# Loads limited to five in flight, two more chunks stacked and one weight tile converted another way, in a linear attention with a gated feed-forward layer

## The chip, the core and the metric

The kernel runs on one core of a Trainium2 chip. A core has five engines with their own instruction queues: TensorE (PE) multiplies matrices, VectorE (DVE), ScalarE (ACT) and GpSimd (POOL) work elementwise, and SyncE (SP) issues nearly all transfers between memory and the core's buffers. PE's weight loads are shown apart as PEld. What counts is the time of one execution in device microseconds; lower is better. An execution's own time is a little more than the span of its trace.

## What is computed

```python
# attention: batch 4, heads 8, 768 tokens, head size 48
for t in range(S):
    kt, vt, rt = k[:, :, t], v[:, :, t], r[:, :, t]
    cur = einsum('bhd,bhe->bhde', u * kt, vt)
    y[:, :, t] = einsum('bhd,bhde->bhe', rt, state + cur)
    state = w * state + einsum('bhd,bhe->bhde', kt, vt)
# feed-forward on x = y with the heads side by side: width 384, 1024 hidden
h = maximum(x @ w_in, 0)
u, v = h[..., :512], h[..., 512:]
v_n = (v - mean(v)) / sqrt(var(v) + 1e-6)
v_s = einsum('ts,bsd->btd', w_spatial, v_n) + b_spatial
out = (u * v_s) @ w_out
```

The two weights w_in and w_out come as 64-bit numbers, all else as 32-bit ones.

## The kernel before

The 4 batches of 768 tokens are cut into 24 chunks of 128 tokens (`m`), six for each batch. A chunk is loaded in four pieces: `rk` (r and k with the head dimension on the partitions), `rs`, `ks` (r and k with tokens on the partitions) and `rkv` (v). `prep` scales them on POOL and DVE, `scores` and `products` multiply in 16 small fp32 matmuls each (two PE records a matmul), `state` carries the recurrence, and `apply` forms the chunk's rows of x in PSUM tile `xp`; `fin` splits x into a high and a low part. The first `FIRST_CHUNKS` chunks come in one form (tensor `rkvE`): `apply` then runs 36 or 48 small matmuls, separately for the carried state and the own chunk, and `block` copies the state into the tile `A` kept for that. The later chunks are stacked (tensor `rkvL`): the state is copied into `rkv`, r and the scores are copied side by side into a tile `A` (`move`, which ACT, DVE or a transfer on SP can do), and `apply` needs 32 matmuls.

The feed-forward products use a high and a low part of each operand, three matmuls a product (`mm3`): `moe_v` and `moe_u` multiply x by w_in, `moe_sp` the normalised v by w_spatial, `moe_out` the gated tile by w_out. w_in is loaded in six tiles (`wa`, three for v first) and w_spatial in six (`wb`); all w_spatial tiles are split into two parts ahead of the first `moe_sp`. `from_f64` (line 459) makes the two parts of a 64-bit weight tile. For tiles in `SUM_IN` (the first three of w_in) it sums three terms in three PE matmuls (lines 479 to 481), for the others it adds on DVE (lines 486, 488, 490).

Which engine does a task, and in which order each engine's instructions stand, is decided while the program is built, by `Plan` (line 118). It keeps a clock for each engine, buffers and the transfers, and takes the ready task with the earliest start, by due times. `SEEDS` shakes these due times and the leanings by random amounts, once for each seed. `Fetch` and `landing` are its models of PE's instruction loading and of loads. `lane` (line 208) lets the planner's loads start no earlier than the eighth last has landed. On the chip SP's queue is in order: a load that waits for its buffer or for an earlier transfer holds whatever stands behind it.

Of the kernel before, what the change touches and what calls it, by code (L numbers as in the profile page):

```python
# [25 lines left out]
NK = DM // P  # L26
# [6 lines left out]

OK, OV = DM, 2 * DM
ROW_E, ROW = OV + 2 * NP * 2 * D, OV + 2 * 2 * NP * HC
FIRST_CHUNKS = 8
SUBS = ((0, 64, 0), (1, 0, 64))


# [1 line left out]
AHEAD = 0.3  # L41
ALONE = 1000.0
CALM, LATE = 80.0, dict(DVE=1.0, SP=1.0)
SEEDS = (286629, 121708, 598343, 820393, 863996, 502042, 154941, 497759, 664270, 626866, 362431, 249003, 459248,
# [4 lines left out]
BIAS = dict(DVE=3.0, ACT=3.5)  # L49
MOST_IN, MOST_OUT = 2, 1  # L50

# [3 lines left out]
CHAIN = dict(PE=0.0, DVE=0.115, ACT=0.11, POOL=0.0, SP=0.0)  # L55
SWITCH = {"bs": 0.095, "br": 0.095, "by": 0.095, "sb": 0.215, "sy": 0.11, "rb": 0.105, "yb": 0.105}
STAY = 1.0
PORT = dict(DVE=(0.07, 0.0, 0.0), POOL=(0.15, 0.06, 0.02))


class Way:
    def __init__(self, engine, cost, emit, two=False, nbytes=0, lean=0.0, behind=None):
        self.engine, self.cost, self.emit, self.two, self.nbytes = engine, cost, emit, two, nbytes
        self.lean = lean + BIAS.get(engine, 0.0)
        self.behind = BEHIND[engine] if behind is None else behind
# [30 lines left out]
class Fetch:  # L96


    FIRST, BLOCK, BASE, SLOPE, MOST = 91, 128, 3.15, 0.5, 2.6

    def __init__(self):
        self.done, self.ready = 0, 0.0
# [15 lines left out]
class Plan:  # L118
# [1 line left out]

    RATE, SLOW, FIRST_BYTE, LANES = 400e3, 210e3, 1.2, 8

    def __init__(self, slots):
        self.slots = {k: [(0.0, i) for i in range(n)] for k, n in slots.items()}
        self.hold = []
        self.slot, self.turn, self.order, self.given, self.since = {}, {}, {}, {}, {}
        self.tasks, self.wrote, self.read, self.users = [], {}, {}, {}
# [41 lines left out]
    def shake(self):  # L171
        for seed in SEEDS:
            rnd = random.Random(seed)
            share, size = rnd.choice((0.01, 0.03, 0.1, 0.3)), rnd.choice((1.0, 3.0, 8.0))
            width, at = rnd.choice((3.0, 12.0, 50.0, 1000.0)), rnd.uniform(-10.0, 330.0)
            for t in self.tasks:
                if abs(t.due - at) < width and rnd.random() < share:
                    t.due += rnd.uniform(-size, size)
                    for w in t.ways:
                        w.lean += rnd.uniform(-size, size)  # L180
# [14 lines left out]
    def shared_cost(self, way, at):  # L195
        if not way.two:
            return way.cost
        lead, gap, tail = PORT[way.engine]
        return max(way.cost, self.port + gap - at + way.cost - lead)
# [6 lines left out]
    AHEAD_IN = 25.0  # L206

    def lane(self, at, landed):
        return max(at, landed[-self.LANES]) if len(landed) >= self.LANES else at

    def run(self):
        self.dues()
# [5 lines left out]
        free, line, landed, clock, fetch, bank = {}, 0.0, [], Clock(), Fetch(), {}  # L218
        self.port, self.kind = 0.0, "b"
        while ready:  # L220
            best, ahead = {}, dict(free)
            for t in sorted(ready, key=lambda t: (t.due, t.place)):
# [7 lines left out]
                for way in t.ways:  # L230
# [4 lines left out]
                    at = max(can, ahead.get(e, 1.0)) if len(t.ways) > 1 else max(can, free.get(e, 1.0))  # L235
                    if way.nbytes:
                        at = max(self.lane(at, landed), t.due - self.AHEAD_IN)
# [3 lines left out]
                _, e, can, way = found  # L241
                at = max(can, free.get(e, 1.0))
                if way.nbytes:
                    at = max(self.lane(at, landed), t.due - self.AHEAD_IN)
                if can <= ahead.get(e, 1.0) + AHEAD and not way.nbytes:
                    ahead[e] = max(can, ahead.get(e, 1.0)) + way.cost
                late = at <= free.get(e, 1.0) + 0.02
                due = t.due - STAY if e == "PE" and (t.kind == "b") == (self.kind == "b") else t.due
                key = (0, due, t.place) if late else (1, at, due, t.place)
# [5 lines left out]
            _, at, t, way = best[e]  # L255
# [6 lines left out]
            if way.two:  # L262
                self.port = at + cost - PORT[e][2]
            if e == "PE":
# [20 lines left out]
            for a in t.after:  # L285
                left[a] -= 1
                if not left[a]:
                    ready.append(a)
            way.emit()
        assert all(t.end is not None for t in self.tasks)  # L290


# [1 line left out]
def fused_kernel(ctx, tc, rkT, rkvE, rkvL, wT, uB, w_in, w_sp, b_sp, w_out, out):  # L294
    nc = tc.nc
    E = mybir.EngineType
    for e in (E.PE, E.DVE, E.Activation, E.Pool, E.SP):
        ctx.enter_context(tc.manual_schedule(engines={e}))
    EARLY, STATS, EC = 13, 1, FIRST_CHUNKS
    QUIET = 6  # L300
    CLASSIC = (0,)
    SUM_IN, SUM_OUT = range(NK), []
    LOAD_IN = {0: -50.0, 1: -50.0}
    SLOTS = dict(rk=2, rs=2, ks=2, rkv=3, a=1, A=2, t=4, X=2, gt=4, u=8, vs=2, g=3, ob=2, pm=5, ps=1, xp=1, x=2, s=2, t1=1, dg=2, q=2)
    SLOTS |= {f"w{x}{n}": 1 for x in "ab" for n in range(NS)}
    const = ctx.enter_context(tc.tile_pool(name="const", bufs=1))
    sbuf = ctx.enter_context(tc.tile_pool(name="sbuf", bufs=1))
    psum = ctx.enter_context(tc.tile_pool(name="psum", bufs=1, space=bass.MemoryType.PSUM))
    plan = Plan(SLOTS)
    T = {}  # L310

    def tile_of(key, shape, dtype=F32):
        key = key[:2]
        if key not in T:
            home = psum if key[0] in ("pm", "ps", "xp") else sbuf
            T[key] = home.tile(shape, dtype, name=key[0], tag=f"{key[0]}{plan.slot[key]}")
        return T[key]
# [33 lines left out]
    def load(key, shape, dtype, src, nbytes, view=None, due=None):  # L351
        def f():
            t = tile_of(key, shape, dtype)
            nc.sync.dma_start(out=view(t) if view else t, in_=src)
        plan.add([("SP", 0.45, f, False, nbytes)], (), [key], lag=0).most = due


# [661 lines left out]
    FIRST = [1, 2, 3, 6, 8, 10]  # L1019
# [121 lines left out]
```

## Time and profile before

| | before |
|---|---|
| time, median of 3 executions | 331.55 us (329.3 to 333.71) |
| the profiled execution | 330.61 us, its span 328.9 us |
| PE busy | 310.1 us, 94% |
| DVE, ACT, POOL busy | 244.9, 194.3, 250.3 us |
| instruction packets of PE's queue | 36, 0.59 MB |
| data moved | 49.73 MB |

The share of busy time is an average over stages; what a wait costs is read where it stands. In the rows below an instruction is given by its line, engine and operation, then the tile written, an arrow, and the tiles read. "issue" as the end of a wait means that the engine waited for nothing that the profile shows.

### The profile page before, as it was taken

The page shows a single profiled execution, that of the slowest core. Times are in us where ns is not written, and L with a number is a line of the kernel's source. Part 1 is how long each engine was busy: PE and PEld are TensorE (multiplying, and loading weights), DVE is VectorE, ACT ScalarE, POOL GpSimd, SP SyncE. Part 2 cuts the span into 40 slices and gives each one's busy share as a digit, 9 for nine tenths or more (in the row PEclk, how much of TensorE's full clock was granted, in tenths as well). Part 3 has the DMA queues.
Part 4 walks back from the last instruction along what each step waited for, and adds up shares of the span by engine and source line. Part 5 has one row for each costly group of instructions (what it writes and reads, how often), then busy time and mean ns, then how long its engine had stood idle before and what let it go on. Part 6 is the DMA issues. An engine that isn't in the chain of part 4 may idle for free.

```text
span 328.9 us, 10946 instructions
## 1 busy us (share of the span) xinstructions
PE 310.1 (94%) x4574; PEld 282.3 (86%) x4574; DVE 244.9 (74%) x469; ACT 194.3 (59%) x481; POOL 250.3 (76%) x235
## 2 busy tenths in 40 slices
PE   2779899999999999999999999999999999999995
PEld 1347788899999898988988999999988998999995
DVE  6889978879892889959999885578999512716840
ACT  5338773654752769667968375675868743533412
POOL 3959879979899889999999876567899730539700
PEclk9989999999999999999999999999999999999999
DMA  7999557666366637343456154243430010100012
GB/s 223 418 410 374 174 199 274 218 226 216 117 209 212 221 113 231 114 151 99 140 178 195 33 185 129 113 150 120 155 136 19 2 72 2 48 24 2 1 50 96
DMA packets 21793, 49.73 MB, mean 151 GB/s; under 512 B 2608, under 2 KB 12528, under 8 KB 21744
## 3 DMA queue, kind: packets, MB, share of 16 engines
q1 hardware_dynamic: 21600, 48.93, 43.2%
q8 instruction: 36, 0.59, 0.8%
q10 hardware_dynamic: 144, 0.10, 0.1%
q14 instruction: 13, 0.11, 0.1%
HBM read 43.58 MB, written 4.72 MB: 147 GB/s over the span
## 4 chain that ended last, share of the span: by engine, by line
PE 57%; POOL 16%; DMA 10%; DVE 9%; issue 4%; ACT 3%; SPq 1%; POOLq 0%; ACTq 0%; DVEq 0%
PE pm L746 15%; PE pm L748 14%; PE pm L747 14%; PE xp L703 5%; DMA ks<-rkvL 5%; DMA rk<-rkT 4%; PE ps L622 3%; POOL t L337 3%; POOL rs L337 2%; POOL X L337 2%; POOL wb L337 2%; POOL u L337 2%; PE ps L641 2%; DMA wa<-w_in 2%; PE pm L479 1%
## 5 line engine op out<-in xcount | busy, mean ns | idle before, releaser
L746 PE MATMUL pm<-wa,t 128*128 128x384 f32 x120 | 41.0, 341 | 0.0
L747 PE MATMUL pm<-wa,t 128*128 128x384 f32 x120 | 40.5, 337 | 0.4 <-POOL wa L337 0.4
L748 PE MATMUL pm<-wa,t 128*128 128x384 f32 x120 | 40.5, 337 | 0.0
L337 POOL TENSOR_TENSOR t<-vs,t 128x384 fp32r<-128x384 f32 x28 | 35.0, 1263 | 5.0 <-ACT t L342 5.0
L746 PE MATMUL pm<-x,wi_h 128*128 128x384 f32 x93 | 31.9, 343 | 0.0
L337 POOL TENSOR_TENSOR a<-diag,dg 128x512 f32<-128x512 f32 x20 | 23.5, 1173 | 10.5 <-ACT A L608 8.0
L748 PE MATMUL pm<-x,wi_l 128*128 128x384 f32 x93 | 31.2, 336 | 0.0
L747 PE MATMUL pm<-x,wi_h 128*128 128x384 f32 x93 | 31.2, 335 | 0.0
L337 POOL TENSOR_TENSOR rs<-rs,ks 128x384 f32<-128x384 f32 x15 | 19.7, 1313 | 11.8 <-DMA ks<-rkvL 4.6
L746 PE MATMUL pm<-wo_h,gt 128*128 128x384 f32 x84 | 28.5, 340 | 0.0
L748 PE MATMUL pm<-wo_h,gt 128*128 128x384 f32 x84 | 28.2, 336 | 0.0
L747 PE MATMUL pm<-wo_l,gt 128*128 128x384 f32 x84 | 28.2, 336 | 0.0
L746 PE MATMUL pm<-wi_h,x 128*128 128x512 f32 x69 | 28.1, 407 | 0.0
L748 PE MATMUL pm<-wi_h,x 128*128 128x512 f32 x69 | 27.3, 395 | 0.0
L747 PE MATMUL pm<-wi_l,x 128*128 128x512 f32 x69 | 27.1, 393 | 0.0
L337 POOL TENSOR_TENSOR gt<-u,gt 128x384 fp32r<-128x384 f32 x20 | 20.9, 1056 | 5.5 <-ACT gt L342 5.4
L337 POOL TENSOR_TENSOR rs<-rs,ub 128x384 f32<-128x384 f32 x22 | 22.7, 1032 | 2.7 <-DVE rs L337 1.9
L608 ACT COPY A<-rk 64x256 f32<-64x256 f32 x50 | 20.2, 405 | 7.3 <-DVE rk L585 2.7
L917 DVE TENSOR_TENSOR g<-pm,bb 128x384 f32<-128x384 f32 x32 | 17.3, 547 | 9.1 <-PE pm L748 7.9
L747 PEld LDWEIGHTS pm<-wa,t 128*128 128x128 f32 x120 | 22.6, 188 | 0.9 <-POOL wa L337 0.7
L746 PEld LDWEIGHTS pm<-wa,t 128*128 128x128 f32 x120 | 22.5, 188 | 0.9 <-issue 0.2
L337 POOL TENSOR_TENSOR ks<-ks,tn 128x384 f32<-128x384 f32 x21 | 23.0, 1094 | 0.0
(180 smaller groups left out, 947.5 us busy)
## 6 DMA issues: line engine op xcount, KB each, us to landing
rk<-rkT SPq DMA_DIRECT2D x24, 512.0 KB, 5.3
rkv<-rkvL SPq DMA_DIRECT2D x16, 512.0 KB, 4.6
out<-ob SPq DMA_DIRECT2D x23, 192.0 KB, 1.9
wa<-w_in SPq DMA_DIRECT2D x6, 512.0 KB, 7.7
rkv<-rkvE SPq DMA_DIRECT2D x8, 384.0 KB, 5.5
rs<-rkvL SPq DMA_DIRECT2D x16, 192.0 KB, 2.5
ks<-rkvL SPq DMA_DIRECT2D x16, 192.0 KB, 5.3
wb<-w_sp SPq DMA_DIRECT2D x6, 384.0 KB, 7.8
```

Source lines behind the costliest of these rows:

```text
L337: plan.add([(e, cost[e], lambda e=e: engine[e].tensor_tensor(**f()), True, 0, lean if e == "DVE" else 0.0) for e in ways.split()], r, w)
L479: nc.tensor.matmul(z(), eye(), h(), start=True, stop=False)
L608: ("ACT", (n + 250) / 1200, lambda out=out, p=p, h=h: nc.scalar.copy(out(), source(p, h))),
L622: nc.tensor.matmul(ps[64 * hf:64 * hf + 64, b, o:o + HC], rk[hd, 1, p, s0:s0 + 64], rk[hd, 0, p, t0:t0 + 64], start=True, stop=True, skip_ ...
L641: nc.tensor.matmul(ps[64 * j:64 * j + D, b, o:o + D], kn[hs, kc:kc + D], ve[hs, h, z, p, slice(0, D) if m < EC else slice(16 * h, 16 * h + ...
L703: nc.tensor.matmul(xp[32 * p:32 * p + 32, o:o + HC], lhsT, rhs, start=p not in began, stop=True, skip_group_check=True, tile_position=(0, ...
L746: nc.tensor.matmul(o, lh, rh, start=first, stop=False, skip_group_check=free)
L747: nc.tensor.matmul(o, lh, rl, start=False, stop=False, skip_group_check=free)
L748: nc.tensor.matmul(o, ll, rh, start=False, stop=last, skip_group_check=free)
L917: dve(TH, lambda: nc.vector.tensor_tensor(out=g(K), in0=T[PM][:, 0:TH], in1=other(), op=ALU.add), [PM, ("c", "bb"), *r], [K])
```

## The change

Five edits. `LANES` becomes a constant of 5, for the planner, and after each emitted load a dependence on the load five before it is added, so that SP waits for that one's end. `FIRST_CHUNKS` goes from 8 to 6, so chunks 6 and 7 are stacked. `SUM_IN` covers the first two tiles of w_in, so the third goes the way without matmuls. `Fetch` has other constants, and `SEEDS` another and longer list.

```diff
-FIRST_CHUNKS = 8
+FIRST_CHUNKS = 6
-SEEDS = (286629, 121708, 598343, 820393, 863996, 502042, 154941, 497759, 664270, 626866, 362431, 249003, 459248,
...
+SEEDS = (956712, 719309, 400612, 159489, 812019, 177741, 597687, 361859, 292312, 116469, 56557, 664906, 436360,
...
+LANES = 5
-    FIRST, BLOCK, BASE, SLOPE, MOST = 91, 128, 3.15, 0.5, 2.6
+    FIRST, BLOCK, BASE, SLOPE, MOST = 92, 128, 3.05, 0.6, 3.1
-    RATE, SLOW, FIRST_BYTE, LANES = 400e3, 210e3, 1.2, 8
-
-    def __init__(self, slots):
+    RATE, SLOW, FIRST_BYTE = 400e3, 210e3, 1.2
+
+    def __init__(self, slots, wait):
+        self.wait, self.sent = wait, []
-        return max(at, landed[-self.LANES]) if len(landed) >= self.LANES else at
+        return max(at, landed[-LANES]) if len(landed) >= LANES else at
-            way.emit()
+            made = way.emit()
+            if way.nbytes:
+                self.sent.append(made.ins)
+                if len(self.sent) > LANES:
+                    self.wait(made.ins, self.sent[-1 - LANES].name)
-    SUM_IN, SUM_OUT = range(NK), []
+    SUM_IN, SUM_OUT = range(2), []
-    plan = Plan(SLOTS)
+    def wait(ins, name):
+        dep = mybir.DependencyInfo(mybir.DependencyClass.Sync, mybir.DependencyReason.DATA)
+        tc.add_manual_dep(ins, name, dep, reason="loads in flight")
+
+    plan = Plan(SLOTS, wait)
-            nc.sync.dma_start(out=view(t) if view else t, in_=src)
+            return nc.sync.dma_start(out=view(t) if view else t, in_=src)
```

Line numbers of the changed kernel are 14 higher than before from `fused_kernel` on.

**Place 1: SP, the first loads.** Before; a name such as DMAHW1 is the semaphore of an earlier transfer, of which eight are used in turn:

```order
L354 DMA rk<-rkT 128x1024
L354 DMA ks<-rkvE 128x384 [waits DMAHW0_49]
L354 DMA wa_132<-w_in 128x1024 [waits DMAHW1_49]
L354 DMA rs<-rkvE 128x384 [waits DMAHW2_49]
L354 DMA rk<-rkT 128x1024 [waits DMAHW3_49]
L354 DMA rkv<-rkvE 128x768 [waits DMAHW4_49]
L354 DMA rkv<-rkvE 128x768 [waits DMAHW5_49]
L354 DMA wa_177<-w_in 128x1024 [waits DMAHW6_49]
L354 DMA wa_186<-w_in 128x1024 [waits DMAHW7_49]
L354 DMA rs<-rkvE 128x384 [waits DMAHW0_49,DVE_49]
```

And of the change, from the fifth transfer on:

```order
L399 DMA ub<-uB 128x384
L368 DMA ks<-rkvE 128x384 [waits DMAHW0_49]
L368 DMA rk<-rkT 128x1024 [waits DMAHW1_49]
L368 DMA rkv<-rkvE 128x768 [waits DMAHW2_49]
L368 DMA wa_157<-w_in 128x1024 [waits DMAHW3_49]
L368 DMA rs<-rkvE 128x384 [waits DMAHW4_49]
L368 DMA rk<-rkT 128x1024 [waits DMAHW5_49]
L368 DMA rkv<-rkvE 128x768 [waits DMAHW6_49]
L368 DMA ks<-rkvE 128x384 [waits DMAHW7_49]
L368 DMA rkv<-rkvE 128x768 [waits DMAHW0_49]
L368 DMA wa_187<-w_in 128x1024 [waits DMAHW1_49]
L368 DMA rs<-rkvE 128x384 [waits DMAHW2_49,DVE_49]
```

The waits begin three transfers earlier, five back in place of eight; the first chunk's rk moved ahead of its rkv, its ks behind rs and the constant ub.

**Place 2: PE, the first chunks.** L479 to L481 are the sums of a w_in tile, L622 scores, L641 products, L703 apply and L769 the first `moe_v`. Before:

```order
L641 MATMUL ps<-rkv,ks 48x48 x16
L622 MATMUL ps<-rk 64x64 x16
L479 MATMUL pm<-wa_100,X 128x512
L480 MATMUL pm<-wi_h,X 128x512
L481 MATMUL pm<-wi_l,X 128x512
L479 MATMUL pm<-wa_132,X 128x512
L480 MATMUL pm<-wi_h,X 128x512
L481 MATMUL pm<-wi_l,X 128x512
L703 MATMUL xp<-rk,A 32x64 x12
L703 MATMUL xp<-a,rkv 32x64 x24
```

Of the change, at the same place (L636 scores, L655 products, L717 apply, L783 `moe_v`):

```order
L636 MATMUL ps<-rk 64x64 x16
L655 MATMUL ps<-rkv,ks 48x48 x16
L493 MATMUL pm<-wa_100,X 128x512
L494 MATMUL pm<-wi_h,X 128x512
L495 MATMUL pm<-wi_l,X 128x512
L717 MATMUL xp<-rk,A 32x64 x12
L717 MATMUL xp<-a,rkv 32x64 x24
L636 MATMUL ps<-rk 64x64 x16
L655 MATMUL ps<-rkv,ks 48x48 x16
L783 MATMUL pm<-wi_h,x 128x512 x6
```

Scores moved ahead of products, and the three matmuls of the third tile are gone.

**Place 3: SP, the loads of chunks 7 to 9.** Of the change; `A<-rk` and `A<-a` (L621) are moves of chunks 6 to 9:

```order
L368 DMA rk<-rkT 128x1024
L621 DMA A<-rk 64x256
L368 DMA rkv<-rkvL 128x1024
L368 DMA ks<-rkvL 128x384
L368 DMA rk<-rkT 128x1024
L621 DMA A<-a 64x512 x2
L621 DMA A<-rk 64x256 x4
L368 DMA rs<-rkvL 128x384
L621 DMA A<-rk 64x256
L368 DMA ks<-rkvL 128x384
L368 DMA rk<-rkT 128x1024
L621 DMA A<-rk 64x256
```

Before, the loads of these chunks stand without moves between them up to the first stacked chunk's:

```order
L354 DMA rk<-rkT 128x1024
L354 DMA rkv<-rkvL 128x1024
L354 DMA ks<-rkvL 128x384
L354 DMA rs<-rkvL 128x384
L607 DMA A<-rk 64x256 x3
```

Moves now stand between loads, where before there were three in a row and then loads again.

## Rows read from the trace of the kernel before

**Rows 1.** The page: engines (busy us, share, instructions), code queue (packets, MB, share).
```profile
PE 310.1 (94%) x4574; PEld 282.3 (86%) x4574; DVE 244.9 (74%) x469; ACT 194.3 (59%) x481; POOL 250.3 (76%) x235
q8 instruction: 36, 0.59, 0.8%
```

**Rows 2.** Stretches: us, busy time of each engine, PE clock, DMA share, GB/s.
```profile
0.00:10.00 10.00, 2.23 (x33) 1.94 (x34) 7.48 (x15) 4.82 (x10) 4.66 (x17) 1.00 0.76 258
10.00:13.30 3.30, 3.30 (x64) 1.61 (x67) 2.49 (x5) 0.59 (x1) 3.30 (x4) 1.00 1.05 419
13.30:21.90 8.60, 5.17 (x138) 3.07 (x129) 8.00 (x16) 3.06 (x7) 5.54 (x6) 1.00 1.03 411
21.90:28.00 6.10, 5.60 (x127) 4.14 (x127) 4.86 (x10) 4.82 (x12) 5.08 (x6) 0.72 1.04 410
28.00:34.50 6.50, 5.29 (x130) 3.81 (x132) 6.36 (x14) 5.59 (x16) 6.26 (x6) 1.00 0.78 278
60.00:150.00 90.00, 89.44 (x1321) 83.13 (x1320) 72.51 (x142) 58.56 (x147) 83.67 (x77) 1.00 0.56 185
```
The engines in each row are PE, PEld, DVE, ACT and POOL.

**Rows 3.** Timeline at the end: start, us, instruction, [idle before, releaser].
```profile
325.43 0.36 DVE L991 COPY ob<-pm 128x192 f32<-128x192 f32 x1 [8.45 <-ACT ob L342]
```

**Rows 4.** Timeline of PE: where it stopped before 45 us.
```profile
21.90 0.58 PE L622 MATMUL ps<-rk 64*64 64x64 f32 x24 [2.42 <-issue]
...
28.02 0.73 PE L769 MATMUL pm<-wi_l,x 128*128 128x512 f32 x2 [0.51 <-issue]
...
34.47 0.87 PE L703 MATMUL xp<-a,rkv 128*32 128x64 f32 x45 [1.07 <-issue]
...
42.76 0.21 PE L622 MATMUL ps<-rk 64*64 64x64 f32 x1 [0.18 <-issue]
```

**Rows 5.** Transfers of PE's code, 19.5 to 20 us: packets, MB, share.
```profile
q8 instruction: 1, 0.02, 11.7%
```

**Rows 6.** The same, 25.5 to 26 us.
```profile
q8 instruction: 1, 0.02, 11.8%
```

**Rows 7.** The same, 32 to 33 us.
```profile
q8 instruction: 1, 0.02, 5.9%
```

**Rows 8.** The same, 36 to 36.5 us.
```profile
q8 instruction: 1, 0.02, 11.6%
```

**Rows 9.** Timeline of SP: the last loads issued before 13.3, 21.9 and 28 us.
```profile
13.07 0.33 SPq L354 DMA_DIRECT2D wb<-w_sp  x1
...
20.56 0.33 SPq L354 DMA_DIRECT2D rkv<-rkvE  x1
...
27.53 0.42 SPq L354 DMA_DIRECT2D wb<-w_sp  x1
```

**Rows 10.** Timeline of POOL and DVE: first operation, and two waits for loads.
```profile
8.31 1.01 POOL L337 TENSOR_TENSOR rs<-rs,ks 128x384 f32<-128x384 f32 x1 [4.33 <-DMA rs<-rkvE]
...
12.66 0.70 DVE L467 TENSOR_SCALAR pm<-wa 128x512 uint32<-128x512 uint32 x1 [0.48 <-DMA wa<-w_in]
...
22.84 1.01 POOL L337 TENSOR_TENSOR rs<-rs,ks 128x384 f32<-128x384 f32 x1 [2.85 <-DMA ks<-rkvE]
```

**Rows 11.** The chain that ended last: apply blocks (start, us, what).
```profile
38.61 1.48 PE xp L703 x96
...
63.34 1.14 PE xp L703 x72
...
153.05 1.03 PE xp L703 x64
```

**Rows 12.** Timeline of PE: the first sum of the third w_in tile.
```profile
16.09 1.14 PE L479 MATMUL pm<-wa,X 128*128 128x512 f32 x2 [1.00 <-PE pm L481]
```

**Rows 13.** Groups by line, DVE and ACT: busy us, mean ns, idle before.
```profile
L488 DVE TENSOR_TENSOR pm<-pm,wa 128x512 f32<-128x512 f32 x3 | 2.1, 690 | 0.0
L608 ACT COPY A<-rk 64x256 f32<-64x256 f32 x50 | 20.2, 405 | 7.3 <-DVE rk L585 2.7 <-DVE rk L581 2.5 <-PE xp L703 1.5
```

**Rows 14.** SP's own waits: us in total, times, longest.
```profile
SPq L607 <- DVE rk L585: 8.4, 1, 8.4
```

11 rows, old and new, of the table SEEDS are left out of this document.

## The prediction

> **What bounds the kernel now.** I read the page first. TensorE (PE) is busy 310.1 of 328.9 us and no other engine over 76% [rows 1], so PE's work plus its idle time is the run, and 18.8 us of it are idle. The table of stretches says where. From 60 to 150 us PE rests 0.6 of 90 us, while GpSimd (POOL) is 93% busy there [rows 2]: PE binds, POOL stands close behind. The last matmul leaves the copies and the store of the last tile from 325.4 us on [rows 3]; the change doesn't touch that tail of 3.5 us. Nearly all the rest lies ahead of 42.8 us, the first ten of them with 2.23 us of work [rows 2]. PE's timeline there shows four stops, of 2.42, 0.51, 1.07 and 0.18 us, each put down to "issue": no engine had to finish anything [rows 4].
>
> The stops are code loading, and they come one by one. Queue q8 carries 36 packets of 0.59 MB, 16 KB each, for 4574 matmuls with as many weight loads: about one packet for 128 matmuls with their loads [rows 1]. Between the stops at 21.90, 28.02 and 34.47 us lie 127 and about 130 matmuls [rows 2]. Counting the program in records (an fp32 matmul leaves two), the first three stops are at records 219, 347 and 475; the edge ahead of them, 91, falls inside the first score block, at 13.3 us. So one block's code seems to be asked for when PE crosses an edge, and needed at the next. The packets ran at 19.5 to 20, 25.5 to 26, 32 to 33 and 36 to 36.5 us [rows 5 to 8], about 2.2 us ahead of each restart, and 6.4, 3.9, 4.2 and 1.8 us after the edge.
>
> What a packet waits for fits what the loads have outstanding. Loads issued minus bytes moved: by 13.3 us, 18 loads (without the 2 KB one) up to the first tile of w_sp, issued at 13.07 us, are 6.95 MB, of which 2.58 + 3.3 x 0.419 = 3.96 had moved: 3.0 MB, 7.3 us at 0.411 MB/us. By 21.9 us 9.44 minus 7.50 is 1.94 MB, 4.7 us. By 28.0 us 11.34 minus 10.0 is 1.34 MB, 3.3 us. By 34.5 us 0.1 MB [rows 2, 9]. Waits of 6.4, 3.9, 4.2 and 1.8 us fall with 3.0, 1.9, 1.3 and 0.1 MB: a packet stands roughly behind what was queued, at some 0.85 of its computed time in the two heaviest cases, and never under 1.8 us.
>
> **Five loads in flight.** Before, the same kind of wait exists eight loads back (the order's DMAHW lanes); now it is five. A load ahead of the first w_sp rows is 0.37 MB on average (6.95 / 18 = 0.39; 0.37 over the first 26 of the new order). Eight make 3.0 MB, which agrees with 13.3 us. Five make 1.85 MB. A part of that has moved and only isn't signalled: the third w_in tile ends 3.28 MB of loads, which had moved at 11.7 us, and its reader starts at 12.66; chunk 2's ks ends 7.14 MB, moved at 21.0, read at 22.84 [rows 2, 10]. Of 1.0 and 1.8 us I take 1.2, which is 0.5 MB. So 1.35 MB, 3.3 us, at 0.85 of that 2.8, plus 2.2 to the restart: **5.0 us a block**. Bounds: 4.1 us, the time from the edge at 38.6 us (the start of the fourth apply block) to the restart at 42.76, where hardly any load stood ahead [rows 4, 11]; above, 8.6, 6.1, 6.5 as now.
>
> Does it starve the queues? The core moves 0.41 MB/us from 10 to 28 us [rows 2]. Five loads of 1.85 MB are 4.5 us of transfer, longer than the 1.0 to 1.8 us between moved and signalled and the 0.3 to 0.4 us of an issue [rows 9], so the rate should hold; the price if it doesn't is the fifth case below.
>
> Instruction order on SP also changes: rk of the first chunk moves ahead of rkv, and chunk 2's ks and rk ahead of most of w_sp. That matters to POOL, which now waits 2.85 us for chunk 2's ks until 22.84 us [rows 10]. In the new order 5.7 MB lie up to that ks instead of 7.14 MB: some 3.5 us earlier at 0.41.
>
> **The startup, worked out.** POOL starts at 8.31 us now, when rs has landed; ks comes one load later in the new order, 0.2 MB or 0.5 us: 8.8 us. POOL's five operations to the scaled ks (1.1, 1.0, 1.25, 1.0, 1.0 by the pitch of such rows) end at 14.1; products and with them the first edge (record 92, 24 records in) at 14.4 us, 1.1 later than now. Then four blocks at 5.0 and one at 4.2 would give 38.6 us for the fifth edge after it (record 732), inside the same product block where PE restarts now at 42.76 us. But VectorE (DVE) allows less: it was idle 0.8 + 0.6 + 1.2 + 0.1 = 2.7 us in 10 to 34.5 us [rows 2], and the third tile adds work there. Walking its new order with a pitch of 0.6 us for 512 columns I get the low half of chunk 2's x at 33.2 us, against 36.45 now, with the next edge at 36 and record 732 at 40.2 us. I take **40.3: 2.4 us gained**. Bounds: 38.5 (4.3 gained), and 43.8 with today's blocks (14.4 + 8.6 + 6.1 + 6.5 + 4.1 + 4.1), 1.0 lost. [...]
>
> **The third tile without sums.** It takes three matmuls off PE, which begin at 16.09 us after a 1.00 us wait [rows 12], the first of them 1.14 us; this lies inside the startup just costed and is not counted twice. DVE loses one operation and gets three of 0.69 us [rows 13], net two: 1.4 us, or 1.2 by the pitch, covered by the 2.7 us of DVE idle time; if that cover is gone it costs up to 1.4 us there.
>
> **Chunks 6 and 7 stacked.** Apply goes from 72 matmuls at 1.14 us (chunk 6 opens a batch) and 96 at 1.48 to 64 at 1.03 each [rows 11]: **0.56 us** off PE, after 43 us, where PE binds. Scores and products keep their counts. ACT gets net 8 copies of r and a at about 0.405 us [rows 13], 12 small ones more and 6 fewer into the state: about 4 us on an engine 59% busy, covered. SP gets five more moves and 0.26 MB more of loads, under idle queues. Bounds: 0 (a move comes late) to 0.56.
>
> **New seeds and the changed planner numbers** reorder everything. Over the whole program POOL gets 6 operations fewer of about 1 us and DVE 10 instructions more; POOL's 93% is thus eased, not tightened. PE's waits between 43 and 325 us are about 2 us in all now; another order can make them 0.5 or 5. I add **0.4 us**, near today's since nothing in the order says otherwise.
>
> Sum: 330.61 us (the profiled execution, span 328.9) - 2.4 - 0.56 + 0.4 = **328.0 us**. The profiled execution is 0.9 below the median of 331.55, so against that median this is 1.1% less.
>
> [...] The trace shows q8's packets 6.4 us behind an edge with 3.0 MB queued and 1.8 with 0.1 [rows 2, 5, 8, 9]. [...]
>
> **Rivals.**
> 1. Code blocks come no faster: another cause than the backlog sets 8.6, 6.1 and 6.5 us. For it: three waits are few, and the third is longer than its bytes. Record 732 at 43.8 us: 330.6 + 1.0 - 0.6 = 331.0 us.
> 2. The lead is given back at POOL: the first spatial products need all six tiles split, most of it on POOL, and POOL hardly rests after 60 us. Against: it starts chunk 2 earlier. Only the 0.56 stays: 330.0 us.
> 3. All of it works: blocks at 4.1 us, 4.3 gained, 0.56, and 1.4 of the later waits gone: 324.3 us.
> 4. Slower: the moves of chunks 6 and 7 block SP. Nine of the moves now stand among the loads of chunks 7 to 9, and SP is in order: one such move already held SP 8.4 us for DVE [rows 14]. If two of them hold chunk loads by some 5.5 us each beyond their slack, POOL and then PE stand: 328.0 + 11 = 339 us. It decides only if more than 10 us of waiting reach PE; against it, the stores and moves that held SP now cost PE almost nothing: it rests 0.6 of 90 us with that 8.4 us wait in the run.
> 5. The five-deep queue starves: at 0.35 instead of 0.41 MB/us, the 10 MB of the first 28 us come 4 us late; 2.4 gained becomes 1.6 lost: 332 us.
>
> **Numbers.** Forecast 0.48 (326 to 330), rival 1 0.18, rival 2 0.11, rival 3 0.13, rival 4 0.06, rival 5 0.04. A difference under 2% is about what a measurement of this kernel can't tell from none. Faster by over 2% means under 324.9 us: rival 3 and a little of the forecast, 0.15. Slower (over 338.2): rival 4 and a rest, 0.07. Within 2%: 0.78. The range 324 to 332.5 leaves out rival 4, half of rival 3 and the worst of rival 5.
>
> **What would show it.** Right: PE's "issue" stops before 45 us sum under 2.5 us (4.2 now), q8's packets run about 3 us after an edge, PE passes the product block of chunk 4 near 40 us, no stretch of 0.5 clock near 24 us, POOL starts chunk 2 near 19.6 us. Wrong: stops of 2 us or more again (rival 1); POOL or DMA as releaser of PE waits near 65 to 75 us (rivals 2 and 4); under 0.38 MB/us in 10 to 28 us (rival 5).

## The result and the profile after

The changed kernel takes **334.75 us** (median of 4 runs, 333.8 to 337.0) against 331.5 us for the kernel before: a ratio of **1.015 [1.011, 1.019]**. It became slower by 1.5%, where the forecast was 328.0 us and the range ended at 332.5 us. The profiled execution took 335.06 us, its span 333.1 us. The sum had started from the one profiled execution, 0.9 us under the median of 331.55; from that median it comes to 329.0. (Medians are over all executions, ratios leave out those more than 1.5% above the fastest of their kernel, and limit alone, repeat of the change and POOL less were profiled in such a one, so that of them only the times are told.)

The page of the changed kernel, engines and code queue (before: [rows 1]):

```profile
PE 310.8 (93%) x4530; PEld 283.6 (85%) x4530; DVE 249.8 (75%) x476; ACT 198.2 (60%) x494; POOL 248.5 (75%) x229
q8 instruction: 35, 0.57, 0.7%
```

PE shows 44 matmul records fewer and yet is busy 0.7 us longer; its idle time went from 18.8 to 22.3 us. The stretches of the changed kernel (us, PE, PEld, DVE, ACT, POOL, PE clock, DMA share, GB/s), and the second of them in the kernel before:

```profile
0.00:44.00 44.00, 30.01 (x728) 22.01 (x728) 36.23 (x70) 23.68 (x59) 32.37 (x44) 0.96 0.89 307
44.00:90.00 46.00, 42.41 (x758) 38.46 (x754) 35.64 (x80) 28.34 (x76) 39.29 (x38) 1.00 0.76 237
```
```profile
44.00:90.00 46.00, 45.20 (x907) 41.64 (x907) 38.22 (x79) 27.63 (x72) 41.07 (x39) 1.00 0.62 206
```

From 44 to 90 us PE now rests 3.6 of 46 us, before 0.8: 2.8 us. The rest is ahead of 44 us. PE's larger stops there and behind, in the timeline of the changed kernel (lines stand 14 higher than before; L717 applies the state, L655 makes the products):

```profile
26.77 0.57 PE L655 MATMUL ps<-rkv,ks 64*48 64x48 f32 x30 [1.85 <-issue]
...
35.43 0.87 PE L717 MATMUL xp<-a,rkv 128*32 128x64 f32 x40 [3.75 <-issue]
...
44.26 0.48 PE L655 MATMUL ps<-rkv,ks 64*48 64x48 f32 x23 [0.21 <-issue]
...
49.91 0.30 PE L717 MATMUL xp<-a,rkv 128*32 128x64 f32 x4 [0.73 <-issue]
...
66.81 1.14 PE L717 MATMUL xp<-A,rkv 128*32 128x64 f32 x64 [1.32 <-DMA A<-a]
...
77.57 1.10 PE L717 MATMUL xp<-A,rkv 128*32 128x64 f32 x64 [1.07 <-DMA A<-a]
```

Two things are to be seen. The stops for code ahead of 45 us are 5.8 us, where they were 4.2 [rows 4] and should have been under 2.5; record 732 falls at 44.3 us instead of 40.3. And the two stacked chunks, 6 and 7, each begin with a wait for a copy into A, 2.4 us in all, where 0.56 us were to be saved.

Of the signs named in advance, the wrong ones came: a code stop of 3.75 us (rival 1), a DMA as what ended PE's waits at 66.8 and 77.6 us (the place of rivals 2 and 4), and 362 GB/s in 10 to 28 us, where the kernel before has 412 (rival 5):

```profile
10.00:28.00 18.00, 15.73 (x348) 10.53 (x347) 15.55 (x31) 7.59 (x20) 14.96 (x15) 1.00 0.99 362
```

### The profile page after: what moved, and what is told of

Same layout as the page of the kernel before. It is cut to its first block, busy times and chain, and to the rows that moved or that the text cites. A ratio compares the mean times of both kernels' runs of the same rounds, so it can differ in the third digit from the quotient of the medians.

```text
span 333.1 us, 10900 instructions
## 1 busy us (share of the span) xinstructions
PE 310.8 (93%) x4530; PEld 283.6 (85%) x4530; DVE 249.8 (75%) x476; ACT 198.2 (60%) x494; POOL 248.5 (75%) x229
## 4 chain that ended last, share of the span: by engine, by line
PE 58%; POOL 11%; DVE 11%; DMA 8%; issue 7%; ACT 4%; SPq 1%; POOLq 0%; DVEq 0%; ACTq 0%
PE pm L760 16%; PE pm L762 16%; PE pm L761 16%; DMA rk<-rkT 5%; PE xp L717 5%; POOL rs L351 3%; PE ps L636 2%; PE ps L655 2%; DVE rk L599 2%; DMA wb<-w_out 2%; POOL rk L593 2%; DMA ks<-rkvE 2%; POOL gt L351 1%; DVE rs L351 1%; POOL t L351 1%
## 5 line engine op out<-in xcount | busy, mean ns | idle before, releaser
L351 POOL TENSOR_TENSOR t<-vs,t 128x384 fp32r<-128x384 f32 x25 | 29.8, 1204 | 2.3 <-ACT t L356 2.3
L351 POOL TENSOR_TENSOR rs<-rs,ks 128x384 f32<-128x384 f32 x18 | 23.3, 1292 | 9.1 <-DMA ks<-rkvE 5.2
L622 ACT COPY A<-rk 64x256 f32<-64x256 f32 x58 | 23.5, 404 | 8.5 <-PE xp L717 3.5
L351 POOL TENSOR_TENSOR gt<-u,gt 128x384 fp32r<-128x384 f32 x23 | 25.9, 1136 | 2.6 <-ACT gt L356 2.6
L351 POOL TENSOR_TENSOR t<-X,t 128x384 fp32r<-128x384 f32 x18 | 23.1, 1285 | 6.2 <-ACT t L356 6.2
L351 POOL TENSOR_TENSOR X<-vs,X 128x384 f32<-128x384 f32 x10 | 11.9, 1187 | 17.0 <-ACT vs L842 16.6
L717 PEld LDWEIGHTS xp<-A,rkv 128*32 128x32 f32 x1152 | 17.0, 110 | 7.1 <-issue 6.8
```

The lines of the kernel that those rows point to most:

```text
L351: plan.add([(e, cost[e], lambda e=e: engine[e].tensor_tensor(**f()), True, 0, lean if e == "DVE" else 0.0) for e in ways.split()], r, w)
L622: ("ACT", (n + 250) / 1200, lambda out=out, p=p, h=h: nc.scalar.copy(out(), source(p, h))),
L717: nc.tensor.matmul(xp[32 * p:32 * p + 32, o:o + HC], lhsT, rhs, start=p not in began, stop=True, skip_group_check=True, tile_position=(0, ...
```

## Experiments

Where an order is called "replayed", the kernel follows a table of all steps (task and engine) as the planner had made them, so that one part changes and no other row moves, but for what the part itself adds; line numbers then stand higher. What the expectations on kernels in the old order call "chunk 5's scores" is the fifth score block, chunk 4 in a count from 0.

A code packet's wait is counted from the start of PE's edge record (91, 219, 347 in the old order, 92, 220, 348 in the new one) to the quarter of a microsecond in which the packet runs. Where PE stopped at the edge, that record stands ahead of the stop at the second and third edges of the old order and behind it at the third of the new one. Which of the two is the moment of the request no trace shows, so such waits are compared within one order only. The prediction counted from behind the stops; hence its 3.9 and 4.2 us for the kernel before, where 6.2 and 5.0 stand below.

**The limit and the copies in the changed kernel.** First the limit taken out, in the order as it is:

```
-                if len(self.sent) > LANES:
-                    self.wait(made.ins, self.sent[-1 - LANES].name)
```

> The changed kernel without the dependences on the load five back; every instruction stands where it stands in the changed kernel, only SP's eight-back waits are left. Theory A (the limit costs: with five loads in flight the queues move 0.33 to 0.37 MB/us in place of 0.41, loads come late, and PE's 3.75 us stop at 35.4 us follows): 2 to 4 us faster than the changed kernel, about 332, 0.41 MB/us in 10 to 30 us. Theory B (the limit helps the code blocks, the order and the moves cost): 1 to 4 us slower than the changed kernel, about 337, with stops of PE for code like those of before, 2 us and more each.

Measured: 335.57 us, ratio 1.011 [1.004, 1.018]. The rate rose from 355 to 383 GB/s in 14 to 34 us, and PE's code stops ahead of its record 732 were 5.4 us, with the limit 5.8. In the new order the limit neither shortens the stops nor costs anything that can be measured.

SyncE's copies as ScalarE copies instead (`nc.scalar.copy(out(), source(p, h))` in the SP way of `move`), once with the limit and once without. The limit counts SyncE's copies as loads too, so each of them takes one of the five places; on ScalarE they take none:

> The changed kernel with its 14 moves that SP issues made by ACT copies at the same places; the rest stands in the same order. If the two waits of PE for a moved tile (1.32 and 1.07 us at 66.8 and 77.6 us) reach the end: 2.0 to 2.4 us faster than the changed kernel, about 332.5. If PE loses the same time elsewhere, since ACT or POOL then binds: within 0.7 us of it.

> Both edits in the changed kernel: no dependences on the load five back, and the moves by ACT. Theory A with moves: the two gains add up, 4 to 6 us faster than the changed kernel, about 330. Theory B: about 335, the gain of the moves spent on longer code stops.

Measured: 333.92 us, 1.0075 [1.003, 1.012], and 334.75 us, 1.010 [1.006, 1.014]. With the limit, the profiled span fell by 1.5 us to 331.6 and the waits on DMA copies into A went, with one new wait of 0.9 us for ScalarE. The medians fall by 0.8 us with the limit and by as much without it (335.57 to 334.75); the intervals overlap, so these two runs don't show that the copies are part of the loss. The runs with stacking in the old order, below, do.

**The limit alone**, in the old order (the same wait, five loads back):

> The kernel before, in its own order, with the dependence on the load five back added and nothing else. Theory A: 1 to 3 us slower than before, about 333, under 0.38 MB/us in 10 to 28 us. Theory B (the forecast's own step): the code packets run about 3 us after an edge in place of 6.4 and 3.9, and it is 1 to 3 us faster than before, about 329.

Measured: 333.75 us, 1.005 [1.0005, 1.009]. A small loss.

**Three in flight instead of five**, new order:

```
-                if len(self.sent) > LANES:
-                    self.wait(made.ins, self.sent[-1 - LANES].name)
+                if len(self.sent) > 3:
+                    self.wait(made.ins, self.sent[-1 - 3].name)
```

> The changed kernel in its own order with three loads in flight instead of five. Theory B (the forecast: the packet waits for the bytes that are out at its request): 0.8 MB out instead of 1.0 to 1.3, so packets 2 to 2.5 us after the request instead of 3.5, 4.1 and 6.2, no stop for code over 0.5 us before 45 us; loads at 0.25 MB per us instead of 0.33, which costs 4 to 8 us elsewhere: median 337 to 342. Theory N (the packet's wait is not set by how many loads are in flight): waits of 3.5 us or more on the first three blocks, with the same late loads on top.

Measured: 350.57 us, 1.055 [1.047, 1.063]. The packets came 2.0, 5.3 and 1.5 us after the requests: shorter in two of three, as the forecast's theory B has it. The price is larger than I set it. The stretch from 14 to 34 us in the kernel before run again, in the changed kernel and with three in flight (last column GB/s):

```profile
14.00:34.00 20.00, 16.57 (x422) 11.46 (x418) 17.59 (x35) 13.38 (x34) 15.59 (x16) 0.91 0.95 377
```
```profile
14.00:34.00 20.00, 15.47 (x406) 11.15 (x402) 18.34 (x36) 11.21 (x30) 14.85 (x15) 1.00 1.00 355
```
```profile
14.00:34.00 20.00, 14.78 (x314) 10.32 (x315) 14.21 (x29) 7.49 (x20) 12.04 (x13) 0.85 0.79 253
```

With three, DVE and POOL lose 4.1 and 2.8 us of work in that stretch against five, where POOL waits up to 2.0 us for a load of ks and DVE 2.0 us for one of w_in.

**No loads while the third block is fetched.** In the changed kernel, six loads wait until the scores of chunk 2 end:

```
+HELD = {("rkv", 4): 2, ("ks", 4): 2, **{(f"wb{n}", "sp"): 2 for n in (1, 2, 4, 5)}}
+        for ins, key in zip(self.sent, self.keys):
+            if key in HELD:
+                self.wait(ins, self.scored[HELD[key]])
```

> The changed kernel in its own order, but six loads (rkv and ks of chunk 4, four tiles of w_sp), which SyncE issued from 26.8 to 33.6 us while TensorE's third code block was out, wait until the scores of chunk 2 end (about 30.2 us). Theory L (the block's packet runs behind the loads that move meanwhile, those issued after its request too): the 1.0 MB out at 26.8 us has moved by 29.5, the packet comes at 29.5 to 30.5 instead of 33.0, TensorE's stop of 3.75 us shrinks to under 0.8, its record 476 comes at 32.5 instead of 35.4, and the median is 331.5 to 332.5. Theory F (a block of that stretch takes its 6 us whatever moves): packet after 32, stop of 2.5 us or more, median 334.5 to 336 because loads are late on top.

Measured: 339.97 us, 1.024 [1.017, 1.030]. The code queue in 28.0 to 28.5 us (packets, MB, share), and the timelines of POOL and PE:

```profile
q8 instruction: 1, 0.02, 18.0%
```
```profile
38.93 0.99 POOL L356 TENSOR_TENSOR rs<-rs,ks 128x384 f32<-128x384 f32 x1 [3.60 <-DMA ks<-rkvE]
```
```profile
40.92 0.89 PE L661 MATMUL ps<-rkv,ks 64*48 64x48 f32 x32 [4.09 <-POOL ks L356]
```

Both theories miss the time. The packet came 1.0 us after the request at 27.0 us, with 0.15 MB of loads out, instead of 6.2 us, and the stop before record 476 was gone. But POOL then stood 3.60 us for one of the six held loads, the ks of chunk 4, which comes ahead of chunk 3's scaled ks in its order, and PE 4.09 us for POOL. That loads which move during a fetch delay it fits this one execution (both waits are counted from behind a stop, here of 2.01 us); taking them away cost more than the stop.

**Both kernels again**, unaltered:

> The changed kernel once more, unaltered. Theory O (its order sets the code waits): packets 3.5, 4.1 and 6.2 us after the requests at records 92, 220 and 348 again, each within 0.7 us, a stop of 3 us or more before record 476, median 334 to 336. Theory V (the waits differ from execution to execution: the kernel of the unstacked chunks, which runs the same rows up to chunk 6, had 2.5, 2.6 and 2.5 us): at least one of the three differs by more than 1 us, the scores of chunk 5 start up to 2 us earlier than 52.1 us, and the median stays at 334 to 336.

> The kernel before once more, unaltered. Theory O: packets 6.3, 6.2 and 5.0 us after the requests, each within 0.7 us; scores of chunk 5 at 41.9 us. Theory V: at least one of the three differs by more than 1 us.

Measured: 336.94 us, 1.016 [1.009, 1.023], and 331.76 us, 1.001 [0.997, 1.005]: the times repeat. The waits don't. The kernel before had packets 6.3, 6.2 and 5.0 us after the requests in the first profile, and 2.9, 5.2 and 5.5 in the second. The first of these has no stop at its edge (13.57 us in the second profile), so nothing in the counting blurs it; its packet in 16.5 to 17 us (first profile: [rows 5]):

```profile
q8 instruction: 1, 0.02, 11.1%
```

Its stops before 45 us in the second (before: [rows 4]):

```profile
20.87 0.47 PE L769 MATMUL pm<-wi_h,x 128*128 128x512 f32 x1 [1.25 <-DVE x L342]
21.84 1.43 PE L769 MATMUL pm<-wi_h,x 128*128 128x512 f32 x5 [0.50 <-DVE x L740]
...
26.68 0.73 PE L769 MATMUL pm<-wi_l,x 128*128 128x512 f32 x2 [1.50 <-issue]
...
35.23 0.69 PE L622 MATMUL ps<-rk 64*64 64x64 f32 x32 [0.47 <-issue]
```

Code took 2.0 us instead of 4.2, and 1.75 us of waits for DVE stand where there were none. Record 731 came at 42.5 us, 0.3 earlier. This is theory V, and it bears on all that follows: a wait read from one profile is one draw.

**The third tile alone**, old order replayed (`SUM_IN, SUM_OUT = range(2), []`):

> The kernel before, its order replayed step by step, with only the third tile of the first weight converted without sums on TensorE (three matmuls fewer, two VectorE operations more). Theory E (the forecast: VectorE's two operations lie in its idle time, TensorE loses 1.1 us of work in a stretch in which it waits for code at its next edge anyway): within 0.5 us of before, 331 to 332. Rival G: the longer VectorE chain makes the first moe_v and chunk 1 late: 332.5 to 333.5. Rival H: TensorE's 2.1 us (1.14 of work, 1.00 of wait) reach the end: 329.5.

Measured: 332.03 us, 0.999 [0.9945, 1.003]. As the forecast had it: nothing either way.

**Stacking alone**, old order replayed, the copies by SyncE (`FIRST_CHUNKS = 6`, and a rule that puts each copy behind its source):

> The kernel before, its order replayed step by step, with only chunks 6 and 7 stacked: twelve copies into A by SyncE, each right behind the step that makes its source, 64 and 64 matmuls instead of 72 and 96. Theory S (the forecast): 0.56 us less on TensorE, 331.0, bounds 0 and 0.56. Theory M (the copies come late on SyncE's queue, as in the changed kernel, where TensorE waited 1.32 and 1.07 us for A): TensorE waits 1 to 2.4 us before the products of chunks 6 and 7, median 332 to 333.5.

Measured: 335.84 us, 1.012 [1.0065, 1.018]: slower, and by more than either theory. The timeline of this kernel around chunk 6: DVE ends a, SyncE issues its two copies, PE waits; then the transfers of 58 to 66 us (KB each, median us from issue to landing):

```profile
56.92 0.73 DVE L725 COPY_PREDICATED a<-mask,ps 128x512 f32<-128x512 uint32 x1
```
```profile
58.58 1.10 SPq L662 DMA_DIRECT2D A<-a  x2
```
```profile
65.44 1.94 PE L758 MATMUL xp<-A,rkv 128*32 128x64 f32 x64 [2.91 <-DMA A<-a]
```
```profile
rkv<-rkvL SPq DMA_DIRECT2D x1, 512.0 KB, 6.2
A<-a SPq DMA_DIRECT2D x2, 128.0 KB, 6.6
```

SyncE issues the copies 0.9 us after a is there, behind three loads of chunk 9, and they land 6.6 us later, as late as the loads beside them. Here a copy of 128 KB inside the chip took the landing time of the load traffic. The wait also cost more than its length: with the granted clock at 0.66 in 65 to 70 us, the 64 matmul records behind it take 1.94 us, where they take 1.10 in the next kernel. The stretches of 44 to 90 and 65 to 70 us here:

```profile
44.00:90.00 46.00, 43.09 (x738) 40.19 (x736) 34.48 (x76) 26.76 (x72) 37.37 (x36) 0.96 0.72 223
65.00:70.00 5.00, 4.56 (x134) 4.37 (x135) 3.32 (x14) 3.68 (x8) 3.62 (x4) 0.66 1.04 335
```

PE rests 2.9 of the 46 us, which is this wait and no other; before, 0.8.

**Stacking with the copies on ScalarE**, old order replayed (`steps.insert(at + 1, (t, "ACT"))` in place of `"SP"`), and the same with the third tile:

> The kernel before, its order replayed step by step, with only chunks 6 and 7 stacked, their twelve copies into A on ScalarE (8 x 0.41 and 4 x 0.62 us) instead of as DMAs. Theory D (the loss of 1.2% with SyncE's copies is their landing: 4 to 5 us after the issue, behind loads): no wait for A of 0.5 us or more, the 0.56 us of matmuls saved come through, median 330.5 to 331.5. Theory R (stacking loses anyway, because ScalarE's four state copies per chunk and rk's buffers come later): 333 or more.

> As the kernel with the stacking on ScalarE, and the third tile converted without sums on TensorE. If both parts are worth what theory says (0.56 us, and the ratio of 0.9986 that the third tile alone had): 330.2 to 331, ratio 0.997. If one of them brings a new wait: 332 or more.

Measured: 331.21 us, 1.001 [0.998, 1.0045], and 332.82 us, 1.004 [1.001, 1.008]. PE's timeline of the first, where chunk 6 begins, with no wait:

```profile
62.42 1.10 PE L758 MATMUL xp<-A,rkv 128*32 128x64 f32 x64
```

So the stacking's 1.2% is the price of its DMA copies (theory D). The two runs differ in the engine of the copies alone, and the late landing with the slower clock behind it makes 3.75 us (2.91 and 0.84) of the 4.6 between their medians. The saving of 0.56 us doesn't show in the time; the interval would allow a gain of that size. The version with the third tile missed its expected 330.2 to 331; its profile has the kind of new wait that the expectation names, for POOL, 0.30 us in the other:

```profile
73.36 0.44 PE L802 MATMUL pm<-wa,t 128*128 128x384 f32 x1 [1.23 <-POOL wa L392]
```

No version here is shown to beat the kernel before.

**Unstacked**, new order replayed (`FIRST_CHUNKS = 8`; the copies of chunks 6 and 7 left out of the table):

> The changed kernel, its order replayed step by step, but chunks 6 and 7 unstacked again (the changed kernel's twelve copies into A for them left out, 72 and 96 matmuls instead of 64 and 64). Theory M (the late copies cost more than the stacking saves): the waits of 1.32 and 1.07 us on A before the products of chunks 6 and 7 go, 0.56 us of matmuls come back, so the profiled span falls by 1.5 to 2, median 333.0. Theory S (the forecast: the stacking is worth 0.56 us and the waits would only stand elsewhere): the median rises to 335.3.

Measured: 340.30 us, 1.024 [1.0175, 1.030]: both theories miss. DVE's and PE's timeline of this kernel say why:

```profile
81.65 0.69 DVE L642 TENSOR_TENSOR rk<-rk,pm 128x512 f32<-128x512 f32 x1 [5.24 <-DMA rk<-rkT]
```
```profile
82.86 0.69 PE L807 MATMUL pm<-wa,t 128*128 128x384 f32 x1 [3.00 <-DVE g L978]
```

An unstacked chunk holds its rk tile until its apply block has read it, and rk has two buffers. The replayed order counts on the stacked chunk, which gives rk up as soon as it is copied; now the load of the next rk comes late, DVE stands 5.24 us at it and PE 3.00 us behind DVE. Up to chunk 8's scores, at 75.5 us, this kernel was ahead of the changed one (78.6 us); of these 3.1 us, 2.1 were there at chunk 5 already, where the two run the same rows. The run tells of rk's buffers, and gives no clean price for stacking.

**POOL less**, old order (three multiplications by ub not emitted):

> The kernel before in its own order, with POOL's multiplication by ub left out for chunks 2, 3 and 4 (three of 1.01 us; the result for those chunks is another). Theory K (POOL's chain sets the stretch from 22.8 to 45 us, in which it has 1.1 us of idle time; code stops lie beside it): chunk 5's scores start 2 to 3 us earlier than 41.6 to 42.1 us, that is at 39 to 40, and the median falls to 328.5 to 330. Theory C (the forecast: TensorE's code stops set it): chunk 5's scores within 0.5 us of 41.9, median 331 to 332.

Measured: 330.68 us, 1.001 [0.997, 1.005]. Theory K falls: 3 us of POOL's work less change nothing that shows. POOL's chain alone doesn't set the startup, no more than the code stops do.

**The new seeds taken back** in the changed kernel, so that the planner makes yet another order:

> The changed kernel with the seeds of the kernel before: limit, stacking, third tile and the planner's constants stay, and the planner makes another order. Theory P (the order found by the new seeds is what the other parts need; an order that no search picked has several late loads): 338 to 345. Theory Q (the seeds move nothing that matters): 333 to 336.5.

Measured: 351.50 us, 1.063 [1.0555, 1.071], more than theory P gave. PE's waits behind the first microseconds are spread: 3.0 us for POOL's rk, 2.6 for DVE's a, 2.6 for POOL's wb, 1.8 for copies into A.

**Limit, stacking and third tile in the old order**, replayed; of the change only the new order is missing:

> The kernel before, its order replayed, with the limit of five, the stacking (copies by SyncE) and the third tile together; of the change only the new order is missing. If the parts add up (ratios 1.0047, 1.0121 and 0.9986 alone): 1.0154, that is 336.5, about the changed kernel's own ratio, and the new order is worth nothing net. If the new order is worth something: 338 to 342 here, against 334.75. If the new order costs: 332 to 334 here.

Measured: 339.21 us, 1.025 [1.019, 1.031]. The three ratios alone give 1.0154; together they cost 0.97% more, and the new order wins back 4.5 us of that (334.75). PE's timeline:

```profile
19.83 1.50 PE L767 MATMUL xp<-a,rkv 128*32 128x64 f32 x48 [2.93 <-DVE a L734]
...
33.90 0.69 PE L686 MATMUL ps<-rk 64*64 64x64 f32 x32 [0.34 <-issue]
...
68.80 1.22 PE L767 MATMUL xp<-A,rkv 128*32 128x64 f32 x64 [3.32 <-DMA A<-a]
```

Here the limit does to the code what the forecast wanted: packets at 3.4, 1.5 and 1.8 us, one stop of 0.34 us left. And chunk 0's a comes late, PE waits 2.93 us for it, and record 731 is 2.6 us later than in the kernel before.

## Why the prediction was wrong

**The step that failed: the startup's 2.4 us.** It had two legs. Five loads in flight were to shorten the code blocks to 5.0 us, and a walk along DVE's chain at its pitch, with no term for waits on loads, POOL or PE, then set record 732 at 40.3 us.

The start of it came nearly as worked out: the first edge at 14.3 us (14.4 forecast), POOL at chunk 2's work at 20.7 us (19.6 forecast, 22.8 before). Then the blocks took 5.7, 6.9, 8.7 and 5.7 us, because the packets came 3.5, 4.1 and 6.2 us after their requests and not 2.8. The walk had the low half of chunk 2's x done at 33.2 us. In the changed kernel it is done at 38.0, since DVE waited for apply matmuls behind PE's stop of 3.75 us; in the unstacked kernel, with the same rows and the same limit up to there and 0.9 us of code stops in all, at 35.6. DVE in the changed kernel, then in the unstacked one:

```profile
36.35 0.56 DVE L356 CAST x<-xp 128x384 fp32r<-128x384 f32 x1 [2.10 <-PE xp L717]
...
37.42 0.55 DVE L754 TENSOR_TENSOR x<-xp,x 128x384 fp32r<-128x384 f32 x1
```
```profile
35.05 0.54 DVE L801 TENSOR_TENSOR x<-xp,x 128x384 fp32r<-128x384 f32 x1
```

Record 732 came at 44.3 us in the one and 42.2 in the other. Of the 4.0 us that it is late, 2.1 went with 4.9 us of code stops; the other 1.9 stay even with hardly a stop, beside 4.2 us of PE's waits for POOL, DVE and ACT, for which the walk had no term. These are single executions. The unstacked kernel had just what was asked for, stops under 2.5 us, and was still only 0.6 us ahead of the kernel before.

**A code stop saved isn't time saved.** For the executions of these startups, the idle times before PE's rows from 13 us up to record 731 (old order) or 732 (new), added up, those for code and all others apart, and the time of that record; where the third tile has no sums, the record that stands for the same work, three matmuls earlier:

| order, kernel | code us | other us | record at us |
|---|---|---|---|
| old: before | 4.2 | 1.0 | 42.8 |
| old: before again | 2.0 | 1.9 | 42.5 |
| old: third tile alone | 1.2 | 3.7 | 43.0 |
| old: stacking alone | 0 | 4.8 | 42.7 |
| old: stacking on ScalarE | 2.4 | 2.6 | 41.4 |
| old: stacking on ScalarE, third tile | 1.2 | 3.8 | 41.8 |
| old: three parts, limit of five | 0.3 | 6.2 | 45.4 |
| new: changed kernel | 5.8 | 0.6 | 44.3 |
| new: copies on ScalarE | 5.7 | 0.7 | 44.5 |
| new: no limit | 5.4 | 0.7 | 43.3 |
| new: no limit, copies on ScalarE | 6.2 | 0.6 | 46.1 |
| new: unstacked | 0.9 | 4.2 | 42.2 |
| new: six loads held | 2.5 | 6.9 | 48.2 |
| new: three in flight | 1.3 | 10.3 | 52.8 |

In the old order without the limit, code stops go from 0 to 4.2 us and the record stays within 41.4 to 43.0. What is not waited for code is waited for DVE and POOL. Stacking alone had no code stop in these 42 us and was 0.1 us ahead of the kernel before. In the new order the stops are not mere cover: with 0.9 us of them the record came at 42.2 us, with 5.4 to 5.8 at 43.3 to 44.5, with 6.2 at 46.1. There a microsecond of stops less brought between a quarter and three quarters of one, in single executions. This is rival 2 in its kind (the lead is given back), though earlier than I put it, within the startup itself and to DVE as well as POOL. The work of POOL alone is no better account of it (POOL less); what exactly, of loads, DVE and POOL, sets 42 us stays open.

**Waits in step with the backlog: failed.** Three waits in one execution made a line. With 2.8 to 3.0 MB out at the first edge, the packet took 6.3 us in one execution of the old order and 2.8 to 3.1 in five others (before again and the four replays without the limit). With 1.0 MB out at the third edge of the new order it took 6.2, with 0.85 it took 2.5 (unstacked, the same rows up to there). Loads seem to matter, as 1.0 us with hardly any suggests; how much they have queued when the request is made doesn't give the wait. A packet came after 2.9 us with some 3 MB out, which alone would take 7 us at the 0.412 MB/us that the kernel before moved in 10 to 28 us, so it did not stand behind all of them; why other executions have waits of 5 to 6 us no run shows.

**The rate: failed too, without being the cause shown.** I held that five loads keep 0.41 MB/us. In 10 to 28 us the changed kernel moved 0.362, against 0.412 before. In 14 to 34 us the rates were 0.374 to 0.377 without the limit in the old order, 0.345 with five there and 0.355 in the changed kernel, 0.25 with three. Rival 5 took 0.35 and gave 332; it was given 4 in 100. In the old order the limit with its companions costs 2.6 us by record 731; in the new order it costs nothing that shows, where the ratios with and without it (1.015 and 1.011) have intervals that overlap.

**Chunks 6 and 7 stacked: the term had the wrong sign.** -0.56 us stood there, at worst 0 if a move comes late, on the ground that SyncE's queues were idle. The issue is quick enough: with stacking alone the copies of a go out 0.9 us after their source. Their landing isn't: 5.1 and 6.6 us for 128 KB in the changed kernel and in the one with stacking alone, beside loads. PE waited 2.4 and 2.9 us. The bound that was missing is a DMA's landing time in that stretch, which the trace of before had: in 58 to 66 us its loads of rk, rkv and ks took 6.6 to 7.3 us from issue to landing, its rs 2.6 (KB each, median us):

```profile
rk<-rkT SPq DMA_DIRECT2D x1, 512.0 KB, 6.6
rkv<-rkvL SPq DMA_DIRECT2D x1, 512.0 KB, 7.3
rs<-rkvL SPq DMA_DIRECT2D x1, 192.0 KB, 2.6
ks<-rkvL SPq DMA_DIRECT2D x1, 192.0 KB, 6.8
```

Rival 4 had the right place and the wrong mechanism: it looked for loads held up behind copies, and it was the copies that came late behind loads.

**The third tile: right, by itself.** 0.999 [0.9945, 1.003], with two DVE operations more. Beside the stacking on ScalarE the ratio was 1.004 [1.001, 1.008], within the noise of the 1.001 without it.

**The new order: 0.4 us, and it can't be told by itself.** With the other three parts fixed, the old order replayed gives 339.2, another set of seeds 351.5, the new one 334.75. The order isn't a term of a few tenths beside the parts; it is what decides whether they cost 1.5 or 6%.

In sum, of the 4.2 us between the two profiled spans (3.3 between the medians), 1.5 are the startup's (record 732 at 44.3 instead of 42.8), and 2.7 come behind it, where the two waits for A are 2.4 and another code stop 0.7. That these waits reach the end is shown for stacking in the old order and not in the new one.

## What to carry to other kernels

A stop on the busiest engine is worth its length only if nothing else would stop the engine in its place: profile the same kernel twice, and if the stop shrinks while the end of the stretch stays, the stop was a cover and not the path. Here it was one in the old order, and in the new order 4.9 us of stops less brought 2.1. A copy inside the chip that went by DMA cost here the landing time of the load traffic around it (5 to 7 us for 128 KB), and on ScalarE 0.4 to 0.6 us of work. Before a limit on transfers in flight is put in, ask what the engines fed by them wait for: in the old order the version with the limit had 3.9 us less of code stops, and its startup ended 2.6 us later.

## What the hardware showed

- A 16 KB code packet took 1.0 us from the end of PE's stop with hardly a load out (0.15 MB), and 2.8 to 6.3 us from the first edge of the old order with some 3 MB of loads out, from one execution to the next, while the medians of the kernel before stayed between 331.15 and 331.76 us.
- The rate of loads by number in flight, 14 to 34 us: 253 GB/s at three, 334 to 355 at five (the run with held loads aside), 363 to 383 with no limit added.
- After the changed kernel's stop of 3.75 us, PE's granted clock was 0.50 of full in 36 to 39 us and 1.00 in 39.5 to 44 us (0.74 in 34 to 38, 0.83 in 38 to 42); in 14 to 34 us it was 1.00. The kernel before had 0.50 in 23 to 26 us, behind its stop of 2.42 us. After the 2.9 us wait of stacking alone it was 0.66 in 65 to 70 us.
